# Block 2's query-key products added over chunks on GpSimd, values ahead of the second softmax, and three blocks' outputs added to x by accumulating DMA

## The chip, the cores and the metric

The kernel runs on one core of a Trainium2 chip. The core has five engines with instruction streams of their own: TensorE (PE: matrix products, with weight loads listed as PEld), VectorE (DVE), ScalarE (ACT), GpSimd (POOL) and SyncE (SP, which here only issues DMAs). SBUF is the on-chip memory of 128 partitions; PSUM holds 8 banks of 128 x 512 float32 in which PE leaves its results. The metric is the device time of one execution in microseconds; a smaller one is better. The median of the runs of the kernel before is 271.93 us.

## The reference

The batch is 1, S = 2048 positions, D = 640 channels, H = 32 heads of Dh = 20, W = 8 offsets, F = 1536 hidden channels, all bf16. Two branches work on the same normalised x, and both are added to x:

```python
def _A_ref(x, wqkv, wo):
    q, k, v = heads(x @ wqkv)          # each [B, H, S, Dh]
    off = jnp.arange(8) * 2
    idx = pos[:, None] - off[None, :]
    ...
    logits = jnp.einsum("bhsd,bhswd->bhsw", q, kg) * scale
    logits = jnp.where(mask[None, None, :, :], logits, -1e9)
    attn = _softmax(logits, axis=-1)
    o = jnp.einsum("bhsw,bhswd->bhsd", attn, vg)
    return o.transpose(0, 2, 1, 3).reshape(B, S, D) @ wo

def _B_ref(x, w_gate, w_up, w_down):
    g = jnp.einsum("bsd,df->bsf", x, w_gate)
    u = jnp.einsum("bsd,df->bsf", x, w_up)
    return jnp.einsum("bsf,fd->bsd", g * u, w_down)

xn = _layernorm(x, axis=-1)
return x + _A_ref(xn, A_wqkv, A_wo) + _B_ref(xn, B_w_gate, B_w_up, B_w_down)
```

So each position attends to eight earlier positions of its own head, two apart, and a gated product without a nonlinearity runs beside it.

## The kernel before

The 2048 positions are cut into NJ = 4 blocks j of 512, each block into 4 tiles of 128 positions (16 tiles t in all). The 640 channels are NCH = 5 chunks c of 128, and the hidden channels are NF = 12 tiles m of 128. Data lies transposed, channels on partitions, positions along the free axis.

**How the order is made.** The code does not emit instructions in the order in which it is written. Each stage is a Python generator that yields conditions (`have`, `num`: a mark or a count has been reached) and Tasks (engine, priority, banks needed). A planner keeps a model time for each engine and picks the next Task per engine by priority; what it picks is the fixed order of that engine's instructions. On the chip semaphores enforce only the data dependencies. Each engine works strictly in that order: an instruction that waits holds up all that stand behind it. `occ` and `acc` are the planner's assumed durations, and `prio` its priorities.

**The stages**, with the names that the instructions bear:

1. Front: LayerNorm of the 16 tiles, transposed by DMA into XNT.
2. Projections (L671, L703): q into `p0_...`, k into `p1_...`, v into `pv...`; values go to a scratch tensor in DRAM (`vst`) and come back shifted as VX (`vx_loads`, 4 DMAs for each of the 20 units u = (block, chunk)).
3. Query-key products. `QUAD`, at L415, says which blocks take the wide way. The narrow way (L835, products at L846, `prod`) multiplies a chunk of q by four shifted views of k on DVE, 128 x 2048 in bf16: two such instructions (r = 1, 0) for each chunk. The wide way (L876) is used for chunks 0 to 3 of a block: DVE multiplies q, read from a PSUM bank, by two shifted views into float32, 128 x 1024 (L893, `prow`), and the four chunks are added into one: by POOL adds (L919 `qsum`, L937 `qend`) and by accumulating DMAs from SBUF to SBUF issued by POOL (L915; `BY_DMA` names the two of four per pair of chunks). For a block on the wide way that is 16 half-products, 8 POOL adds and 4 DMAs. Chunk 4 always goes the narrow way. In before, block 3 alone is wide.
4. Logits (L944): matmuls at L959 sum over the 20 channels of each head with the small selector G, 32 output rows at a time, four column groups side by side. A narrow block needs 2 x 5 x 4 = 40 of them, a wide one 16.
5. Softmax over the eight offsets, L986, in two halves: x = 0 for blocks 0 and 1, x = 1 for blocks 2 and 3, on DVE with the exponential on ACT (L1007) and the last multiply `attn` at L1016; then 16 small DMAs move the weights into ATX0 or ATX1.
6. Weighted values (L1077, L1093): for each unit two multiplies on DVE (L1131, `pv`) into float32 PV, each followed by one add on POOL (L1136, `pva`) into an SV slot; then a selector matmul on PE over all units of a batch (L1174, matmuls at L1184, named I0 to I19), evicted into OT by ACT (L1193). `BATCH`, L1049, lists the last unit of each batch. First and last chunks of a block are multiplied in halves, because ACT must replace the weights in PSUM between blocks (L1091).
7. Gate and up (`gu`, L1206): 5 matmuls for each of 12 tiles m, twice, per block (L1235); ACT evicts the gate (L676), DVE multiplies by the up bank (L1244, `h`), or ACT evicts both and POOL multiplies (L1261, `hp`). Results lie in HT for blocks 0 and 1, in HX for block 2 and in XNT for block 3 (`ht`).
8. Down and output projection (`dn`, L1290, L1302): for each tile t and each half row, 12 matmuls over the hidden tiles and 5 over OT into one bank (L1317); DVE adds x from XR (L1330, `fin`) into FOUT, and SP stores the row. XR is loaded by `xr_loads` (L1278), three slots in turn.

Where PE would have nothing to do in attention, the planner fills it with stage 7. The selector matmuls of stages 4 and 6 run in a mode with four column groups; all others use the whole array.

Of the kernel before, what the change touches and what calls it, by code (L numbers as in the profile page):

```python
# [6 lines left out]
ALU = mybir.AluOpType  # L7
# [13 lines left out]
NJ = 4  # L21
# [327 lines left out]
def build_kernel(nc, A_x, A_wqkv, A_wo, B_x, B_w_gate, B_w_up, B_w_down, out):  # L349
# [39 lines left out]
    NS = 5  # L389
    SV = [sb(f"SV{i}", [128, 4, JB], at=a_pr + i * 4096) for i in range(3)]  # L390
    SV += [sb("SV3", [128, 4, JB], at=a_qk + 33024), sb("SV4", [128, 4, JB], at=a_qk + 33024 + 4096)]
    SV += [sb(f"SV{5 + i}", [128, 4, JB], at=a_ra + i * 4096) for i in range(3)]
    sv_free = [3, 4, 0, 1, 2]
    a_sc = place[0]
    place[0] += 8192
# [16 lines left out]
    NPR = len(PRD)  # L412
    PRD += [sb("PRD12", [128, 4, JB], at=a_sc), sb("PRD13", [128, 4, JB], at=a_sc + 4096)]
    PRD32 = [K.sbuf(f"PRF{i}", [128, 2, JB], FP32, K.base[p.name]) for i, p in enumerate(PRD)]
    QUAD = {3: (1, 0)}  # L415
    BY_DMA = (((0, 0), (0, 2)), ((1, 0), (1, 2)))
    NXR = 3
    a_xr = place[0]
    XR = sb("XR", [128, NXR, D])
    FOUT = sb("FOUT", [128, 2, D])  # L420
    NXN = 5
    XNS = sb("XNS", [128, NXN, D], at=a_xr)
    NUX = 3
# [14 lines left out]
    def ht(j, m):  # L438
        if j == 3:
            return XNT[:, m % NCH, m // NCH * JB:(m // NCH + 1) * JB]  # L440
        return HX[HXM[m]][:] if j == 2 else HT[:, j, m, :]

    HXM = (0, 1, 2, 3, 8, 9, 10, 11, 4, 5, 6, 7)
    WPOS = (2, 0, 1)
# [57 lines left out]
    def loads():  # L502
        def t(f, *a):
            return Task("sp", lambda: f(*a), prio=0)

        for t_ in range(3, NXS):
            yield t(x_load, t_)
        yield t(wqkv_load, 2)
        for t_ in range(NXS, NT):
            yield have("apply", t_ - NXS)  # L510
            yield t(x_load, t_)

        def w(T, src):
            dma(T[:], src.rearrange("(c p) n -> p c n", p=128), w=[T[:]], name="ld_w")

        def pads():
            z = ZERO[:, 0:PAD].unsqueeze(1).to_broadcast([128, NCH, PAD])
            dma(vscr[:, 0:PAD].rearrange("(c p) s -> p c s", p=128), z, r=[ZERO[:, 0:PAD]], w=[("vscr", "pad")], name="vpad")

        yield have("xnt", NT - 1)  # L520
        yield t(w, WG, B_w_gate)
        yield t(pads)
        yield t(w, WU, B_w_up)

    def late_loads():
        yield num(NJ, "lg")
# [519 lines left out]
        yield Task("sp", move, r=[L[:]], prio=4)  # L1046

    NU = NJ * NCH
    BATCH = (4, 9, 14, 19)  # L1049

    def vx_loads():
        yield have("products")
# [121 lines left out]
    def sums(us):  # L1174
        hold = []
        for u in us:
            yield have("add", u)

        def go(*bs):
            hold.extend(bs)  # L1180
            for u, b in zip(us, bs):
                for dq in range(4):
                    o, p = PS[32 * dq:32 * dq + 32, b, :], SV[sv_of[u]][:, dq, :]
                    op("pe", (lambda o, p, dq: lambda e: e.matmul(o, SEL[:], p, start=True, stop=True,  # L1184
                                                                 tile_position=(0, 32 * dq)))(o, p, dq),
                       r=[SEL[:], p], w=[o], name=f"I{u}_{dq}", occ=0.054, lat=0.4, mode=1)
                sv_free.append(sv_of[u])

        def ev():
            for u, b in zip(us, hold):  # L1190
                j, c = divmod(u, NCH)
                o = OT[:, j, c, :]
                X = op("act", (lambda o, b: lambda e: e.activation(o, PS[:, b, :], ACT.Copy))(o, b), r=[PS[:, b, :]], w=[o],  # L1193
                       name=f"oev{u}", occ=0.58)
                K.free_bank(b, X)
                bump("ot", j)

        yield Task("pe", go, r=[SV[sv_of[u]][:] for u in us], prio=9.7, banks=len(us), slack=0.7)
        yield Task("act", ev, r=[PS[:, b, :] for b in hold], prio=3)
# [6 lines left out]
    def gu(j):  # L1206
        if j == 0:
            for m in range(NCH):
                for jj in range(NJ):
                    yield num(4, "qk", 1, jj, m)  # L1210
            for jj in range(NJ):
                yield num(NCH, "v", jj)
        elif j == 1:
            for m in range(NCH):
                for jj in range(NJ):
                    yield num(4, "qk", 0, jj, m)
        elif j == 2:
            yield have("atx", 0)
        if j:
            yield have("gu", j - 1)  # L1220
        for m in range(NF):
            h = ht(j, m)
            if j == 1 and m == 6:
                yield num(NJ - 1, "lg")
            if j == 2 and m == 4:
                yield num(NJ, "lg")
            if j == 2 and m == 8:
                yield have("atx", 1)
            hold = []

            def go(which, b):
                T = (WG, WU)[which]
                for c in range(NCH):
                    l, x = T[:, c, m * 128:(m + 1) * 128], XNT[:, c, j * JB:(j + 1) * JB]
                    op("pe", (lambda l, x, c: lambda e: e.matmul(PS[:, b, :], l, x, start=(c == 0), stop=(c == NCH - 1)))(l, x, c),  # L1235
                       r=[l, x], w=[PS[:, b, :]], name=f"gu{which}_{m}_{j}_{c}", occ=0.2158, lat=0.3)
                hold.append(b)

            def after(h=h, hold=hold, j=j, m=m):
                def ev():  # L1240
                    K.free_bank(hold[0], evac([(h, PS[:, hold[0], :], JB)], f"gev{m}_{j}"))

                def mul():
                    X = op("dve", lambda e: e.tensor_tensor(h, h, PS[:, hold[1], :], ALU.mult), r=[h, PS[:, hold[1], :]],  # L1244
                           w=[h], name=f"h{m}_{j}", occ=0.65)
                    K.free_bank(hold[1], X)
                    bump("h", j)

                yield Task("act", ev, r=[PS[:, hold[0], :]], w=[h], prio=7)
                yield lambda: len(hold) > 1  # L1250
                if on_pool(j, m):
                    k = ucount[0] % NUX
                    k0 = ucount[0]
                    ucount[0] += 1
                    us = UX[:, k, :]

                    def uev():
                        K.free_bank(hold[1], evac([(us, PS[:, hold[1], :], JB)], f"uev{m}_{j}"))

                    def pmul():  # L1260
                        op("pool", lambda e: e.tensor_tensor(h, h, us, ALU.mult), r=[h, us], w=[h], name=f"hp{m}_{j}",  # L1261
                           occ=1.15, lock=True)
                        bump("hp")
                        bump("h", j)

                    yield Task("act", uev, r=[PS[:, hold[1], :]], w=[us], prio=7)
                    yield num(k0, "hp")
                    yield room(1.15)
                    yield Task("pool", pmul, r=[h, us], w=[h], prio=HP_PRIO, lock=True)
                    return  # L1270
                yield Task("dve", mul, r=[h, PS[:, hold[1], :]], prio=H_PRIO)

            yield Task("pe", lambda b: go(0, b), prio=50, banks=1, keep=GU_KEEP, r=[WG[:]])
            K.spawn(after())
            yield Task("pe", lambda b: go(1, b), prio=49, banks=1, keep=GU_KEEP - 1, r=[WU[:]])
        mark("gu", j)

    def xr_loads():  # L1278
        yield num(NJ, "lg")
        yield have("vx", NVX)  # L1280
        for t in range(NT):
            if t >= NXR:
                yield have("out", t - NXR)
            yield Task("sp", lambda: dma(XR[:, t % NXR, :], xhbm[t * TS:(t + 1) * TS, :], w=[XR[:, t % NXR, :]], name=f"xr{t}"),
                       prio=15, w=[XR[:, t % NXR, :]])
            mark("xr", t)

    stores = []
# [1 line left out]
    def dn(j):  # L1290
# [3 lines left out]
        for st in range(4):  # L1294
            t = 4 * j + st
            pieces = ((0, 320), (320, 480), (480, 640)) if t == NT - 1 else ((0, 320), (320, 640))
            yield have("xr", t)
            yield lambda: count.get(("ot", j), 0) >= NCH or ("gu", NJ - 1) in done
            for nb, (c0, c1) in enumerate(pieces):
                yield from dn_piece(j, t, nb, slice(st * TS, (st + 1) * TS), c0, c1)  # L1300
# [1 line left out]
    def dn_piece(j, t, nb, rows, c0, c1):  # L1302
# [1 line left out]
        wid = c1 - c0  # L1304
        hold = []
        n = NF + NCH
        o, xr = FOUT[:, t % 2, cols], XR[:, t % NXR, cols]

        def part(lo, hi):
            b = hold[0]  # L1310
# [17 lines left out]
        def fin():  # L1328
# [2 lines left out]
                   name=f"fin{t}_{nb}", occ=0.15 + wid / 960)  # L1331
            K.free_bank(b, X)

        def store():
            if t == NT - 1:
                f, d = o, ohbm[t * TS:(t + 1) * TS, cols]
            else:
                f, d = FOUT[:, t % 2, :], ohbm[t * TS:(t + 1) * TS, :]
            stores.append(dma(d, f, r=[f], name=f"odma{t}_{nb}", eng="act" if nb == 1 and t == NT - 1 else "sp"))

        def tail():
            yield num(NCH, "ot", j)
            yield Task("pe", rest, r=[OT[:, j, :, rows]], prio=40)
            yield Task("dve", fin, r=[PS[:, hold[0], :], xr], w=[o], prio=FIN_PRIO)
            if nb == 1 or t == NT - 1:
                yield Task("act" if nb == 1 and t == NT - 1 else "sp", store, r=[o], prio=9)
# [13 lines left out]
    FIRST = 9  # L1360
    GU_KEEP = 3
    HP_MAX = 2
    ORDER = ((0, "n"), (1, "n"), (2, "n"), (3, "n"), (3, "w"))
    LAST = ORDER[-1][0]
    HP_PRIO = 30
    DN_KEEP = 3
# [79 lines left out]
```

## Time and profile before

| what | value |
|---|---|
| runs of before | 271.67, 271.93, 272.11 us, median 271.93 |
| the profiled execution, its own time | 271.67 us |
| its span | 270.1 us |
| mean granted TensorE clock | 1.0 |
| matmuls L1235 (gate, up), x469 | 116.9 us busy |
| matmuls L1317 (down, output), x357 | 55.0 us busy |
| POOL adds of values L1136 x40 | 93.9 us, mean 2.367 |
| POOL multiplies L1261 | 16 before the last value add, 1.12 to 1.17 us each |
| DVE multiplies of values L1131 x54 | 91.6 us, 2.279 whole and 1.215 half |
| DVE half-products L893 x16 | 18.9 us, mean 1.217 |
| DVE bf16 products L846 x32 | 36.7 us, one taking 1.219 in the mean |
| DVE output adds L1330 x33 | 15.6 us |
| last value add on POOL ends | 239.12 us |
| PE's last matmul ends | 267.36 us |

The span is what the profile covers; 1.57 us of the execution's own time lie around it. Start times are in us from the span's start. In a row of a group the columns are: line, engine, operation, output and inputs with their shapes, count; then the busy time and the mean ns of one; then the idle time just ahead of the group's instructions and what ended most of it. A matmul's end is modelled, and matmuls are pipelined, so the pace (the distance from one start to the next) is the number to use for PE: 1.079 us for a group of five, 2.31 for a piece of 17 with 320 columns.

### The profile page before, as it was taken

The numbers are of one execution on the slowest core, as the hardware profiler recorded it, in microseconds if no ns is written. First come the engines' busy times: TensorE is split into PE (matmuls) and PEld (weight loads), VectorE is DVE, ScalarE is ACT, GpSimd is POOL, SyncE is SP. The second block draws the span as 40 slices with busy tenths as digits, with TensorE's granted clock in tenths as the row PEclk, the third lists the DMA queues.
The fourth block names the chain that finished last, engine by engine and source line by source line (L and its number), as shares of the span: only waits on it lengthen the run. The fifth ranks groups of instructions, "written<-read, shape, count | busy, mean of one in ns | idle before, by whom it ended". The sixth has DMA issues, their size and how long they took to land.

```text
span 270.1 us, 4455 instructions
## 1 busy us (share of the span) xinstructions
PE 261.8 (97%) x1771; PEld 152.5 (56%) x1788; DVE 214.4 (79%) x254; ACT 109.3 (40%) x194; POOL 142.0 (53%) x95
## 2 busy tenths in 40 slices
PE   7999999999998999999899999999999999999996
PEld 5986964544443444444344577446764577544775
DVE  4687899999986989599996979979998999711221
ACT  3459986558524222435534500453006500365000
POOL 3000000000062289993379998799986999775000
PEclk9999999999999999999999999999999999999999
DMA  7964679602429992895222836633567311300101
GB/s 228 368 186 88 125 133 402 209 0 96 124 50 209 224 226 72 247 280 120 57 47 49 201 107 170 182 98 81 146 173 192 80 49 55 93 0 2 49 27 49
DMA packets 40933, 35.75 MB, mean 132 GB/s; under 512 B 16080, under 2 KB 39120, under 8 KB 40912
## 3 DMA queue, kind: packets, MB, share of 16 engines
q1 hardware_dynamic: 40096, 33.31, 45.6%
q0 software_dynamic: 576, 2.10, 3.9%
q8 instruction: 14, 0.23, 0.4%
q10 hardware_dynamic: 240, 0.05, 0.1%
q14 instruction: 7, 0.06, 0.1%
HBM read 25.07 MB, written 5.26 MB: 112 GB/s over the span
## 4 chain that ended last, share of the span: by engine, by line
PE 72%; DVE 9%; ACT 6%; POOL 5%; SPq 3%; issue 2%; DMA 2%; DVEq 0%
PE PS L1235 30%; PE PS L1317 27%; PE PS L671 9%; DVE PRD L846 4%; POOL SV L1136 3%; SPq L467 3%; ACT XNS L582 3%; PE PS L703 2%; PE PS L1184 1%; PE PS L959 1%; DMA XST<-in_A_x_dram 1%; DVE SM L989 1%; DVE LOG L1016 1%; POOL HT L1261 1%; DVE PV L1131 1%
## 5 line engine op out<-in xcount | busy, mean ns | idle before, releaser
L1136 POOL TENSOR_TENSOR SV<-PV 128x1024 bf16<-128x1024 f32 x40 | 93.9, 2367 | 13.8 <-DVE PV L1131 12.1
L1131 DVE TENSOR_TENSOR PV<-VX,PS 128x1024 f32<-128x1024 bf16 (+1 forms) x54 | 91.6, 1727 | 5.8 <-POOL SV L1136 3.9
L671 PE MATMUL PS<-XNT,WQKV 128*128 128x512 bf16 (+2 forms) x384 | 59.8, 315 | 1.7 <-ACT HT L676 1.1
L1235 PE MATMUL PS<-XNT,WG 128*128 128x512 bf16 x237 | 59.0, 379 | 0.5 <-DVE HT L1244 0.2
L1235 PE MATMUL PS<-XNT,WU 128*128 128x512 bf16 x232 | 57.9, 379 | 0.9 <-ACT HT L676 0.5
L671 PEld LDWEIGHTS PS<-XNT,WQKV 128*128 128x128 bf16 x390 | 37.7, 113 | 23.4 <-ACT HT L676 1.6
L1235 PEld LDWEIGHTS PS<-XNT,WU 128*128 128x128 bf16 x240 | 23.2, 98 | 29.3 <-ACT HT L676 1.0
L1235 PEld LDWEIGHTS PS<-XNT,WG 128*128 128x128 bf16 x240 | 23.3, 98 | 28.6 <-DVE HT L1244 0.7
L846 DVE TENSOR_TENSOR PRD<-QT,KT 128x2048 bf16<-128x2048 bf16 x32 | 36.7, 1219 | 0.0
L1330 DVE TENSOR_TENSOR FOUT<-PS,XR 128x320 bf16<-128x320 f32 (+1 forms) x33 | 15.6, 477 | 17.8 <-PE PS L1317 17.7
L1317 PE MATMUL PS<-WD,HT 128*128 128x320 bf16 x192 | 28.4, 299 | 0.0
L1317 PE MATMUL PS<-WO,OT 128*128 128x320 bf16 (+1 forms) x165 | 26.6, 295 | 0.0
L919 POOL TENSOR_TENSOR PRF<-PRF,PRF 128x1024 f32<-128x1024 f32 x4 | 9.4, 2356 | 29.3 <-DVE PRF L893 29.3
L978 POOL MEMSET LOG<- 32x6 bf16 (+6 forms) x7 | 0.4, 95 | 44.1 <-ACT LOG L970 44.1
L1317 PEld LDWEIGHTS PS<-WD,HT 128*128 128x128 bf16 x192 | 18.6, 98 | 7.8 <-DVE HX L1244 0.4
L676 ACT ACTIVATE HT<-PS 128x512 bf16<-128x512 f32 x24 | 13.8, 594 | 22.5 <-PE PS L1235 22.5
L676 ACT ACTIVATE UX<-PS 128x512 bf16<-128x512 f32 x21 | 12.6, 600 | 25.4 <-PE PS L1235 23.5
L893 DVE TENSOR_TENSOR PRF<-PS,KT 128x1024 f32<-128x1024 f32 x16 | 18.9, 1217 | 0.8 <-DMA PRF<-PRF 0.8
L1317 PEld LDWEIGHTS PS<-WO,OT 128*128 128x128 bf16 x165 | 15.9, 98 | 5.9
L676 ACT ACTIVATE HX<-PS 128x512 bf16<-128x512 f32 x12 | 7.2, 597 | 26.7 <-PE PS L1235 26.6
L676 ACT ACTIVATE XNT<-PS 128x512 bf16<-128x512 f32 x12 | 7.2, 597 | 24.9 <-PE PS L1235 24.9
L1244 DVE TENSOR_TENSOR HT<-HT,PS 128x512 bf16<-128x512 bf16 x20 | 13.4, 681 | 4.6 <-ACT HT L676 3.3
(63 smaller groups left out, 248.6 us busy)
## 6 DMA issues: line engine op xcount, KB each, us to landing
VX<-v_scratch SPq DMA_DIRECT2D x80, 130.0 KB, 2.9
XST<-in_A_x_dram SPq DMA_DIRECT2D x16, 160.0 KB, 5.7
v_scratch<-VST SPq DMA_DIRECT2D x4, 640.0 KB, 5.4
XR<-in_A_x_dram SPq DMA_DIRECT2D x16, 160.0 KB, 2.8
out_dram<-FOUT SPq DMA_DIRECT2D x15, 160.0 KB, 2.0
PRF<-PRF POOLq DMA_DIRECT2D x4, 512.0 KB, 8.7
WG<-in_B_w_gate_dram SPq DMA_DIRECT2D x1, 1920.0 KB, 7.7
WU<-in_B_w_up_dram SPq DMA_DIRECT2D x1, 1920.0 KB, 11.5
```

The lines of the kernel that those rows point to most:

```text
L467: return op(eng, lambda e: e.dma_start(o, i), r=r, w=w, dma=True, name=name, nbytes=n, group=group, land=land)
L671: op("pe", (lambda o, l, x, c, first: lambda e: e.matmul(o, l, x, start=first, stop=(c == NCH - 1)))(o, l, x, c, first), r=[l, x], w=[o], ...
L676: X = op("act", (lambda o, i: lambda e: e.activation(o, i, ACT.Copy))(o, i), r=[i], w=[o], name=name, occ=0.12 + n * 0.9e-3)
L846: op("dve", lambda e: e.tensor_tensor(s[:], qb, kv, ALU.mult), r=[q, rk], w=[s[:]], name=f"prod{j}_{r}_{c}", occ=1.15, lock=True)
L893: X = op("dve", lambda e: e.tensor_tensor(o[:], qb, kv, ALU.mult), r=[q, rk, ("qev", j, c)], w=[o[:]], name=f"prow{j}_{r}_{c}_{q0}", occ=1.17)
L919: yield Task("pool", lambda: op("pool", lambda e: e.tensor_tensor(x, x, y, ALU.add), r=[x, y] + tokens(), w=[x], name=name, occ=2.36, lock ...
L1131: op("dve", lambda e: e.tensor_tensor(p, vw, a, ALU.mult), r=[vv] + rk, w=[p], name=f"pv{u}_{x}_{r0}", occ=0.09 + 1.1 * nr)
L1136: X = op("pool", lambda e: e.tensor_tensor(o, p[:, :, 0, :], p[:, :, 1, :], ALU.add), r=[p[:]] + tokens(), w=[o], name=f"pva{u}_{x}", occ= ...
L1235: op("pe", (lambda l, x, c: lambda e: e.matmul(PS[:, b, :], l, x, start=(c == 0), stop=(c == NCH - 1)))(l, x, c), r=[l, x], w=[PS[:, b, :] ...
L1244: X = op("dve", lambda e: e.tensor_tensor(h, h, PS[:, hold[1], :], ALU.mult), r=[h, PS[:, hold[1], :]], w=[h], name=f"h{m}_{j}", occ=0.65)
L1317: op("pe", (lambda l, x, i: lambda e: e.matmul(dst, l, x, start=(i == 0), stop=(i == n - 1)))(l, x, i), r=[l, x], w=[PS[:, b, :]], name=f" ...
L1330: X = op("dve", lambda e: e.tensor_tensor(o, PS[:, b, 0:wid], xr, ALU.add), r=[PS[:, b, :], xr], w=[o], name=f"fin{t}_{nb}", occ=0.15 + wi ...
```

## The change

Four things change together.

- **Block 2 takes the wide way too.** `QUAD` gets block 2, and `ORDER` plans block 2's wide part ahead of block 3's. Block 2 loses 8 of its 10 narrow products and 24 of its 40 logit matmuls, and gets 16 half-products, 8 POOL adds and 4 accumulating DMAs. One narrow pair per block stays (chunk 4).
- **Outputs of blocks 0 to 2.** x is no longer added on DVE. Early on, one DMA on SP copies rows 0 to 1535 of x into the output (`copy_x`, planned after the second block's logits; in SP's order it stands between the stores of values of block 0 and block 1, ahead of the loads of ATX). For blocks 0 to 2 ACT evicts each half row from PSUM into FB0, and when a block's eight pieces are there, one DMA issued by POOL adds the block of 512 rows to the output (`add_out`, `accum_op=add`). Block 3 keeps the way of before (FB1, XR). XR is loaded for block 3's four tiles only, once block 0's down pieces are planned, and SP stores rows of block 3 alone.
- **Batches.** The units' sums go in seven batches instead of four (`BATCH`). Block 3's batches wait until the down pieces of block 2 are planned.
- **Places in SBUF.** Block 2's last four hidden tiles use block 3's OT instead of slots that wait for softmax 2's move, so the wait `have("atx", 1)` of `gu(2)` is gone; SV has six slots instead of eight; the buffers of the outputs move.

In the fixed orders that come out, PE has seven batches of small matmuls for the units: I0, I1 inside block 2's hidden tiles, I2 to I4 after the gate of tile 3 of block 3, then I5 and I6 between down tiles 1 and 2, I7 to I9, I10 and I11, I12 to I14 and I15 to I19 among the further down tiles. Block 2's logits stand after the up product of tile 10 of block 0, block 3's after the gate of tile 11 of block 1. On POOL, all sums of block 2 stand ahead of block 3's, and these ahead of the first value add; eight `hp` stand ahead of the last value add where there were 16, and the three output DMAs stand between the two adds of units 9, 14 and 19.

```diff
-    SV += [sb(f"SV{5 + i}", [128, 4, JB], at=a_ra + i * 4096) for i in range(3)]
+    SV += [sb("SV5", [128, 4, JB], at=a_ra + 6 * D * 2)]
...
-    QUAD = {3: (1, 0)}
+    QUAD = {2: (1, 0), 3: (1, 0)}
     BY_DMA = (((0, 0), (0, 2)), ((1, 0), (1, 2)))
-    NXR = 3
     a_xr = place[0]
-    XR = sb("XR", [128, NXR, D])
-    FOUT = sb("FOUT", [128, 2, D])
+    FB0 = sb("FB0", [128, 5, D])
+    FB1 = sb("FB1", [128, 2, D], at=a_ra)
+    XR = sb("XR", [128, 4, D], at=a_ra + 2 * D * 2)
...
-        return HX[HXM[m]][:] if j == 2 else HT[:, j, m, :]
+        if j == 2:
+            return OT[:, 3, m - 8, :] if m >= 8 else HX[HXM[m]][:]
+        return HT[:, j, m, :]
...
+        def copy_x():
+            a, b = ohbm[0:3 * JB, :], xhbm[0:3 * JB, :]
+            o, i = a.rearrange("(p r) n -> p (r n)", p=128), b.rearrange("(p r) n -> p (r n)", p=128)
+            op("sp", lambda e: e.dma_start(o, i), w=[("outx",)], dma=True, name="outx", nbytes=2e6)
+
+        yield num(2, "lg")
+        yield t(copy_x)
...
-    BATCH = (4, 9, 14, 19)
+    BATCH = (1, 4, 6, 9, 11, 14, 19)
...
+        if us[-1] >= 3 * NCH:
+            yield num(8, "dn", 2)
...
-            if j == 2 and m == 8:
-                yield have("atx", 1)
...
-        yield num(NJ, "lg")
-        yield have("vx", NVX)
-        for t in range(NT):
-            if t >= NXR:
-                yield have("out", t - NXR)
+        yield num(8, "dn", 0)
+        for st in range(4):
+            t = 12 + st
...
-            yield have("xr", t)
+            if j == 3:
+                yield have("xr", t)
...
-        o, xr = FOUT[:, t % 2, cols], XR[:, t % NXR, cols]
+        F, ft = (FB1, t % 2) if j == 3 else (FB0, t % 4)
+        o, xr = F[:, ft, cols], XR[:, t % 4, cols]
...
+        def fin_act():
+            K.free_bank(hold[0], evac([(o, PS[:, hold[0], 0:wid], wid)], f"fin{t}_{nb}"))
+            bump("fin", j)
+            if count["fin", j] == 8:
+                K.one(Task("pool", add_out, r=[F[:, 0:4, :]], prio=5))
+
+        def add_out():
+            d = ohbm[j * JB:(j + 1) * JB, :].rearrange("(t p) n -> p t n", p=128)
+            f = F[:, 0:4, :]
+            stores.append(op("pool", lambda e: e.dma_start(d, f, accum_op=ALU.add), r=[f, ("outx",)], w=[("out", j)], dma=True,
+                             name=f"oadd{j}", occ=0.88, acc=4))
...
+            if j < 3:
+                yield Task("act", fin_act, r=[PS[:, hold[0], :]], w=[o], prio=6)
+                return
...
-    ORDER = ((0, "n"), (1, "n"), (2, "n"), (3, "n"), (3, "w"))
+    ORDER = ((0, "n"), (1, "n"), (2, "n"), (3, "n"), (2, "w"), (3, "w"))
```

More of the change, by code (lines that the diff above doesn't have):

```diff
@@ L1278, in xr_loads @@
     def xr_loads():
-        yield num(NJ, "lg")
-        yield have("vx", NVX)
-        for t in range(NT):
-            if t >= NXR:
-                yield have("out", t - NXR)
-            yield Task("sp", lambda: dma(XR[:, t % NXR, :], xhbm[t * TS:(t + 1) * TS, :], w=[XR[:, t % NXR, :]], name=f"xr{t}"),
-                       prio=15, w=[XR[:, t % NXR, :]])
+        yield num(8, "dn", 0)
+        for st in range(4):
+            t = 12 + st
+            yield Task("sp", lambda: dma(XR[:, st, :], xhbm[t * TS:(t + 1) * TS, :], w=[XR[:, st, :]], name=f"xr{t}"),
+                       prio=15, w=[XR[:, st, :]])
             mark("xr", t)
@@ L1337, in store @@
             else:
-                f, d = FOUT[:, t % 2, :], ohbm[t * TS:(t + 1) * TS, :]
+                f, d = F[:, ft, :], ohbm[t * TS:(t + 1) * TS, :]
             stores.append(dma(d, f, r=[f], name=f"odma{t}_{nb}", eng="act" if nb == 1 and t == NT - 1 else "sp"))
```

## The prediction, made before the change ran

> **What bounds the kernel now.** I read the busy totals first, then the chain that ended last, then windows of that chain's stages (length, then busy us of PE, PE's weight loads, DVE, ACT and POOL, the granted clock, the DMA share, GB/s).
>
> ```profile
> PE 261.8 (97%) x1771; PEld 152.5 (56%) x1788; DVE 214.4 (79%) x254; ACT 109.3 (40%) x194; POOL 142.0 (53%) x95
> PE 72%; DVE 9%; ACT 6%; POOL 5%; SPq 3%; issue 2%; DMA 2%; DVEq 0%
> 35.00:84.00 49.00, 47.33 (x306) 22.98 (x310) 45.55 (x44) 29.78 (x51) 5.05 (x9) 1.00 0.49 153
> 130.00:151.00 21.00, 19.69 (x102) 8.23 (x103) 18.56 (x18) 11.62 (x22) 16.78 (x10) 1.00 0.30 71
> 151.00:249.00 98.00, 97.63 (x644) 58.53 (x647) 77.61 (x69) 28.89 (x53) 87.10 (x46) 1.00 0.41 107
> ```
>
> PE is the bound, at full granted clock. So a change pays only by taking matmuls or gaps out of PE, and costs only where it makes PE wait. After 151 PE has no gap to lose, but POOL is busy 87.1 of 98 us there: it is the next bound. Before 84 POOL is nearly empty (5.05 of 49). PE's few gaps stand in the chain of waits (start, duration, what) and in the timelines:
>
> ```profile
> 45.12 2.27 PE PS L959 x40
> 79.92 1.93 DMA ATX<-LOG
> 81.88 1.12 ACT PS L1091 x2
> 82.99 0.53 ACT HT L676
> 83.56 2.35 PE PS L671 x10
> 111.82 0.98 PE PS L959 x16
> ...
> 136.48 1.15 DVE LOG L1016
> 137.69 4.67 POOL SV L1136 x2
> ```
> ```profile
> 117.92 3.61 DVE L989 TENSOR_TENSOR M<-M 128x512 bf16<-128x512 bf16 x2
> 126.11 3.00 DVE L989 TENSOR_TENSOR SM<-LOG 128x1024 f32<-128x1024 bf16 x1
> 150.38 0.39 PE L1184 MATMUL PS<-SV,SEL 128*32 128x512 bf16 x2 [0.61 <-POOL SV L1136]
> ```
>
> PE stood 1.56 us before 83.56 (softmax 1's weights go by DMA, then two ACT copies, then the eviction that PE needs), 0.98, 0.65 and 0.47 at 131 to 136.5 (its banks wait for DVE, which is in softmax 2), and 1.10 inside the batch of five units' sums near 150 (unit 4's last add on POOL ends 150.32). The matmuls after each gap run a little denser: a block-by-block sum from 83.56 to the end (94 groups of five at 1.079, 33 down pieces at 2.31 less two halves, 96 small ones) leaves 2.1 us of real loss in 183.8.
>
> **The change, part by part.**
>
> *Logits.* A block multiplied in bf16 costs 40 small matmuls (2.27), a block added over chunks 16 (0.98). Block 2 goes from 40 to 16: PE saves 1.3. The batch also moves behind 83.56, so that PE fills the time before it with two groups more.
>
> *Block 2 on DVE and POOL.* Eight products of 128x2048 bf16 (pace 1.137 in a run, mean 1.219) become sixteen half-products of the same price: +9.1 us of DVE, between 69 and 110, where DVE is the fullest engine after PE (45.55 of 49 before 84). What is late by it are the hidden multiplies (0.6 each), and behind them PE's banks; their cover is that the half-products now wait for POOL's buffers, and DVE goes to the multiplies in between. Without that cover one bank would be late by one half-product, 1.1. POOL gets eight more adds and four more accumulating DMAs:
>
> ```profile
> L919 POOL TENSOR_TENSOR PRF<-PRF,PRF 128x1024 f32<-128x1024 f32 x4 | 9.4, 2356 | 29.3 <-DVE PRF L893 29.3
> L915 POOL DMA_DIRECT2D PRF<-PRF x4 | 3.6, 892 | 9.9 <-DVE PRF L893 7.9 <-DMA PRF<-PRF 2.0
> L1131 DVE TENSOR_TENSOR PV<-VX,PS 128x2048 f32<-128x2048 bf16 x26 | 59.1, 2279 | 1.7 <-POOL SV L1136 1.7
> ```
>
> 8 x 2.32 (pace) + 4 x 0.89 = 22.1 of POOL, from 68.95 (the first softmax's end). With the landings (8.3 to 9.4, median 8.7), as block 3 shows them (76.95 to 109.86, which is 32.9, some 2 of it a landing awaited, and DVE's blocks of multiplies in it), block 2 ends near 99.4, 2.4 sooner than that analogy (101.8), because three half-products are made inside the first softmax, ahead of its last operation, and POOL can start at once. PE comes to its logits at 83.56 + 16 groups x 1.079 = 100.8. Covered by 1.4, and late by 1.1 if the analogy holds in full. Block 3's adds then start at 99.4 and are paced by its half-products on DVE (the last near 115): end near 128.7; PE is there after 27 groups and a logit batch more, at 130.9. Covered by 2.2. I take no new gap at the logits, but POOL reaches its first value add 19 us later: unit 0's ends near 131.0, against 112.2.
>
> *Values and softmax 2.* Unit 1's second product ends 5.1 after that add (117.3 now, 136.3 then, with a pending multiply between). From it to the end of the second softmax DVE takes 20.3 now; one product more, 2.2, lies between: 136.3 + 22.5 = 158.8 against 137.62. If the two blocked operations above (3.61 for two, 3.00 for one, against 1.2 in the first softmax) run free because POOL waits meanwhile, 3 us come back: 156 to 160; I take 159, nearest to the row.
>
> From there to unit 4's last add now takes 12.6, with three GpSimd multiplies of 1.12; with two, 11.5: 170.5. PE wants it at 167.8: 83.56 + 75 groups x 1.079 + two logit batches (1.96) + the batch of units 0 and 1 (0.73) + the entry and first two units of the next (0.6). A gap of 2.7, in which the old ones at 131 and 150 are gone. Behind it on PE stand 17 groups (18.3), 33 down pieces (73.8) and 60 small matmuls in five batches (4.7): 96.9. So PE ends at 170.9 + 96.9 = 267.8 against 267.36: +0.5. Without that gap it would be 265.2.
>
> *Seven batches for four.* Entering and leaving the small-matmul mode costs 0.42 gaps on either side, part of which the denser next group gives back: 0.3 net, so +0.9, counted above. The Trainium skill, page "TensorEngine Tiling (Array Packing)", Key Properties, says that changing the tiling mode drains TensorE. This speaks against the change and agrees with the 0.42 seen; by the rule without the give-back three batches would cost 2.5 rather than 0.9.
>
> *POOL from unit 5 to 19.* 30 adds x 2.32 = 69.6, four multiplies (4.5), three issues of the new output DMA. Rows for such an issue: 0.84 to 1.00 for 128 rows of 4 KB. The new one has 512 rows of 1,280 B: if the price goes by call 0.9, if by row 3.5. I take 1.0, near the row, and keep 0.84 to 3.5. Sum 77.1; plus the gaps in which POOL now waits for DVE at block borders (0.23 three times, 1.41, 0.46, 0.23: 2.8), of which I take half, since fins leave DVE: 1.4. Unit 19's add: 170.5 + 78.5 = 249.0. PE wants it at 170.9 + 78.2 = 249.1. In balance, with 0.7 to 1.5 of slack at the earlier batches without the border gaps. I put +0.5 for what of them shows. The output DMA is followed on POOL by the second add of units 9, 14 and 19; it waits for eight ACT copies and the copy of x, both early, so nothing stands long behind it.
>
> *Outputs.* 24 of DVE's 31 half-row adds of 0.487 (11.7 us) become ACT evictions (0.39 for 128x256, about 0.45 here: 11). ACT is busy 28.9 of 98, so hidden; if it were late, PE's next bank would be. SP loses 23 issues. The copy of x rows 0 to 1535 (1.97 MB) goes out on SP after the second logits, ahead of the value stores and the ATX moves; its landing lies under 80 us of other work. Its issue and bandwidth could push the ATX0 wait at 83.56 by 0 to 1; nearest row: 1.9 MB of weights land in 11.5. That delay would be swallowed by the gap at unit 4: 0. The first eviction of block 1 waits for block 0's output DMA to have read its buffer; there are 13 us of cover by the 8.7 landing. Last fins and stores are as now (2.74 after PE's end).
>
> The Trainium skill, page "SBUF — State Buffer", section "Who interferes with whom", says that a VectorE operation with two SBUF inputs and a GpSimd one that reads SBUF exclude each other. The rows 3.61 and 3.00 fit that. Here DVE gets 16 more of the PSUM-fed kind, which the rule lets pass; without the rule their 1.217 beside POOL's 2.36 says the same.
>
> **Sum.** Against the profiled execution (271.67, span 270.1): +0.5 +0.5, and 0.3 for issue and border together = +1.3, so 273.0. The median shown is 271.93.
>
> **Rivals.**
> 1. *Softmax 2 comes early enough.* If attention's last operation ends at or before 156.2 (no blocking by POOL, block 3's adds denser), unit 4's gap goes and POOL gains as much. 271.67 - 2.1 = 269.6, with half the border cost 270.1. For: 6.6 us in the two blocked rows. Against: POOL still adds values through the same softmax.
> 2. *The output DMA's issue is the new bound.* Its place is POOL between units 9, 14 and 19. At 3.5 each it costs 7.5 more than reckoned, against a slack of 0.1 at unit 19; it decides from 1.2 per issue on. At 2.0: +3.0, so 276; at 3.5: 280. For: four times as many rows. Against: no such row in the trace.
> 3. *Block 2's adds or the copy of x make the logits late.* Slack 1.4: if the landings go from 8.7 to 11 with 2 MB more traffic, block 2's sums, block 3's and softmax 2 shift by 2 to 4, and the gap at unit 4 with them: 275.
> 4. *Balance.* Gains and gaps meet within 0.5: 271.7.
>
> **How the numbers follow.** Forecast 0.42, rival 1 0.25, rival 2 0.10, rival 3 0.11, balance 0.12. The likeliest has its own range of 272.2 to 274.2. With rival 1's times and rivals 2 and 3 to 276 the range is 270.0 to 276.0; beyond it, below 270.0 about 0.1 and above 276.0 about 0.1. A measurement of this kernel tells 0.2% (0.54 us) from no change. Faster: rival 1 and a little of balance, 0.27. Same: balance and the forecast's lower edge, 0.15. Slower: the rest, 0.58.
>
> **What would show it.** Right: PE idle at 131 to 136 gone, a gap of 2 to 3 before unit 4's sums released by POOL, attention's end near 159, POOL's last value add near 249, the block logits with 16 matmuls without a wait, and an issue of the output DMA near 1.0. Wrong: no gap at unit 4 (rival 1), POOL busy over 2 us in an output issue (rival 2), PE waiting at logits 2 or 3 for POOL (rival 3), or a new gap at 83.56 beyond 2.6.

## The result, and the profile after

| kernel | median, us | runs | lowest to highest |
|---|---|---|---|
| before | 272.02 | 4 | 271.67 to 272.43 |
| changed | 282.06 | 4 | 280.63 to 282.35 |

The ratio is 1.0358, with a 95% interval of 1.0319 to 1.0397: the change costs some 10 us. The forecast was 273.0 with a range of 270.0 to 276.0, so it missed. The profiled execution of the changed kernel took 280.63, with a span of 278.8; its span is 8.7 longer than that of before.

The page of the changed kernel, its busy line, the slices of the granted clock and the line of the chain by engine:

```profile
PE 262.9 (94%) x1747; PEld 151.8 (54%) x1764; DVE 221.1 (79%) x249; ACT 111.8 (40%) x203; POOL 155.6 (56%) x99
PEclk9999999999997799999999999999999999999999
PE 65%; DVE 14%; SPq 6%; ACT 5%; POOL 4%; DMA 3%; issue 2%; DVEq 0%
```

PE's busy time is 1.1 us up, though it has 24 matmuls less to do: two slices ran at a lower clock. In the chain, PE's share fell from 72% to 65%, and SP's queue went from 3% to 6%. The chain around those slices (start, duration, what):

```profile
69.10 0.73 SPq L469
...
85.23 3.78 DMA ATX<-LOG
89.03 1.12 ACT PS L1101 x2
90.15 0.52 ACT HT L686
...
90.72 10.26 PE PS L1245 x40
...
109.61 0.98 PE PS L969 x16
```

This is the chain that stood before the 1.56 us gap at 83.56, link by link, but 7.2 us later: the 16 moves into ATX0, two copies on ACT, one eviction, and PE. The gap in before's timeline (1.56 is read between PE's weight loads; between its matmuls it is 1.07):

```profile
83.56 1.88 PEld L671 LDWEIGHTS PS<-XNT,WQKV 128*128 128x128 bf16 x10 [1.56 <-ACT HT L676]
```

Two timelines of the changed kernel show where the 7.2 us arise, first ACT, then SP and POOL:

```profile
77.09 0.60 ACT L686 ACTIVATE HT<-PS 128x512 bf16<-128x512 f32 x1 [3.72 <-PE PS L1245]
89.03 1.12 ACT L1101 ACTIVATE PS<-ATX 128x512 f32<-128x512 bf16 x2 [11.34 <-DMA ATX<-LOG]
90.09 1.06 ACT L686 ACTIVATE HT<-PS 128x512 bf16<-128x512 f32 x2
```
```profile
69.10 17.51 SPq L469 DMA_DIRECT2D ATX<-LOG  x16
73.77 1.03 POOL L925 DMA_DIRECT2D PRF<-PRF  x1
75.04 0.85 POOL L925 DMA_DIRECT2D PRF<-PRF  x1 [0.24 <-DVE PRF L903]
78.13 0.84 POOL L925 DMA_DIRECT2D PRF<-PRF  x1 [2.24 <-DVE PRF L903]
81.49 0.85 POOL L925 DMA_DIRECT2D PRF<-PRF  x1 [2.52 <-DVE PRF L903]
```

ACT stood 11.34 us at a copy whose result DVE first uses at 128.7 (the first value product). Behind the copies in ACT's order stood the eviction of gate tile 2, for which PE waited 8.27 us (between matmuls). SP spent 17.51 us on the 16 moves; before it was 11.21:

```profile
69.31 11.21 SPq L467 DMA_DIRECT2D ATX<-LOG  x16
```

The four DMAs that block 2 adds on POOL fall into just this stretch. In before, the DMAs of block 3 were issued from 85.7 on, when the moves had landed (at 81.9):

```profile
85.69 1.00 POOL L915 DMA_DIRECT2D PRF<-PRF  x1 [4.07 <-DVE PRF L893]
```

The windows of the stage (length, then busy us of PE, weight loads, DVE, ACT, POOL, then granted clock, DMA share, GB/s), of after:

```profile
84.00:130.00 46.00, 39.02 (x184) 17.68 (x188) 34.37 (x37) 12.16 (x21) 28.27 (x15) 0.93 0.61 124
```

In before, PE was busy for 45.74 us there, at a clock of 1.00. The two terms that make the loss are the later start (90.72 against 83.56: 7.2) and the slow matmuls right behind it (40 in 10.26 us, where 40 x 0.216 = 8.64: 1.6). 7.2 + 1.6 = 8.8, against 8.7 in the span; all else that the change does adds up to nothing.

In three of the four runs of the changed kernel the mean granted clock was 0.982 and not the 0.988 of the profiled one, and these took 1.2 to 1.7 us more, which the last section comes back to.

### The profile page after: what moved, and what is told of

Same layout as the page of the kernel before. It is cut to its first block, busy times and chain, and to the rows that moved or that the text cites. A ratio compares the mean times of both kernels' runs of the same rounds, so it can differ in the third digit from the quotient of the medians.

```text
span 278.8 us, 4404 instructions
## 1 busy us (share of the span) xinstructions
PE 262.9 (94%) x1747; PEld 151.8 (54%) x1764; DVE 221.1 (79%) x249; ACT 111.8 (40%) x203; POOL 155.6 (56%) x99
## 4 chain that ended last, share of the span: by engine, by line
PE 65%; DVE 14%; SPq 6%; ACT 5%; POOL 4%; DMA 3%; issue 2%; DVEq 0%
PE PS L1327 27%; PE PS L1245 26%; PE PS L681 8%; SPq L469 6%; DVE PRD L856 4%; POOL SV L1146 3%; ACT XNS L592 3%; DVE SM L999 2%; DVE PV L1141 2%; PE PS L713 2%; PE PS L1196 2%; DMA XST<-in_A_x_dram 1%; DMA ATX<-LOG 1%; PE PS L969 1%; DVE PRF L903 1%
## 5 line engine op out<-in xcount | busy, mean ns | idle before, releaser
L1146 POOL TENSOR_TENSOR SV<-PV 128x1024 bf16<-128x1024 f32 x40 | 96.5, 2674 | 12.5 <-DVE LOG L1026 7.8
L1245 PE MATMUL PS<-XNT,WU 128*128 128x512 bf16 x236 | 59.2, 381 | 0.4 <-issue 0.3
L903 DVE TENSOR_TENSOR PRF<-PS,KT 128x1024 f32<-128x1024 f32 x32 | 37.9, 1217 | 0.3 <-PE PS L681 0.3
L929 POOL TENSOR_TENSOR PRF<-PRF,PRF 128x1024 f32<-128x1024 f32 x8 | 18.8, 2358 | 32.0 <-DVE LOG L1026 20.7
L1254 DVE TENSOR_TENSOR HT<-HT,PS 128x512 bf16<-128x512 bf16 x24 | 16.4, 685 | 17.9 <-ACT HT L686 9.5
L856 DVE TENSOR_TENSOR PRD<-QT,KT 128x2048 bf16<-128x2048 bf16 x24 | 27.3, 1222 | 0.0
L686 ACT ACTIVATE FB<-PS 128x320 bf16<-128x320 f32 x24 | 10.5, 438 | 40.1 <-PE PS L1327 40.1
L947 POOL TENSOR_TENSOR PRD<-PRF,PRF 128x1024 bf16<-128x1024 f32 x8 | 18.7, 2357 | 1.6 <-DVE PRF L903 1.6
L1340 DVE TENSOR_TENSOR FB<-PS,XR 128x320 bf16<-128x320 f32 (+1 forms) x9 | 4.1, 455 | 15.4 <-PE PS L1327 15.4
L557 DVE BATCH_NORM_STATS2 STATS<-XST 128x6 f32<-128x320 bf16 x32 | 14.1, 471 | 2.4 <-DMA XST<-in_A_x_dram 2.3
```

The source lines that it names most:

```text
L686: X = op("act", (lambda o, i: lambda e: e.activation(o, i, ACT.Copy))(o, i), r=[i], w=[o], name=name, occ=0.12 + n * 0.9e-3)
L856: op("dve", lambda e: e.tensor_tensor(s[:], qb, kv, ALU.mult), r=[q, rk], w=[s[:]], name=f"prod{j}_{r}_{c}", occ=1.15, lock=True)
L903: X = op("dve", lambda e: e.tensor_tensor(o[:], qb, kv, ALU.mult), r=[q, rk, ("qev", j, c)], w=[o[:]], name=f"prow{j}_{r}_{c}_{q0}", occ=1.17)
L929: yield Task("pool", lambda: op("pool", lambda e: e.tensor_tensor(x, x, y, ALU.add), r=[x, y] + tokens(), w=[x], name=name, occ=2.36, lock ...
L947: yield Task("pool", lambda: op("pool", lambda e: e.tensor_tensor(o, a, y, ALU.add), r=[a, y] + tokens(), w=[o], name=f"qend{j}_{r}_{q0}", ...
L1146: X = op("pool", lambda e: e.tensor_tensor(o, p[:, :, 0, :], p[:, :, 1, :], ALU.add), r=[p[:]] + tokens(), w=[o], name=f"pva{u}_{x}", occ= ...
```

## The experiments

Each was compared with the kernel before on the same chip (medians of before between 272.16 and 272.35). "Copies" are the two ACT instructions at L1101, named atp0_0 and atp0_1, which bring softmax 1's weights into PSUM.

| run | edit against | median, us | ratio to before, 95% |
|---|---|---|---|
| e1_copies_later | changed | 270.66 | 0.9956 (0.9936 to 0.9976) |
| e2_sums_on_pool | changed | 272.35 | 1.0000 (0.9976 to 1.0023) |
| e3_x_copied_later | changed | 281.97 | 1.0351 (1.0309 to 1.0394) |
| e4_before_copies_later | before | 270.34 | 0.9928 (0.9911 to 0.9945) |
| e5_filler | changed | 279.85 | 1.0278 (1.0241 to 1.0314) |
| e6_block3_wide_alone | changed | 272.78 | 1.0023 (1.0013 to 1.0032) |
| e7_no_pool_multiplies | e1 | 268.28 | 0.9854 (0.9838 to 0.9871) |
| e8_units_later | e1 | 271.27 | 0.9984 (0.9965 to 1.0002) |
| e9_before_no_pool_multiplies | before | 268.25 | 0.9854 (0.9835 to 0.9873) |
| e10_block3_wide_no_pool_multiplies | changed | 269.25 | 0.9892 (0.9875 to 0.9909) |
| e11_five_batches | e7 | 267.77 | 0.9836 (0.9819 to 0.9854) |

**e1: does PE stand because of ACT's order?** After planning, the two copies are moved within ACT's list; no other order changes.

```diff
     K.run()
+    at = [X for X in K.ops if X.name in ("atp0_0", "atp0_1")]
+    K.ops = [X for X in K.ops if X not in at]
+    i = [X.name for X in K.ops].index("gev11_0")
+    K.ops[i:i] = at
     K.emit(stores)
```

> The changed kernel with the two ACT copies of softmax 1's weights moved, in ACT's order alone, from ahead of the eviction of gate tile 2 to behind block 2's logits; all else in the same order. Theory (the 8.3 us stand of PE at 82.4 comes from ACT's order: the copies wait for the late ATX0 moves and hold up the evictions behind them): no stand there, no low clock after it, PE at block 2's logits near 99, end near 271 (269.5 to 274, since POOL's sums of block 2 may be late by some us). Rival (PE stands there for work that is late itself, the half-products or the banks): PE stands at the same place or within 10 us behind it for nearly as long, 278 to 282.

It took 270.66, 11.4 less than the changed kernel. The ATX0 moves were nearly as slow as in the changed kernel (16.58 us, the last of them issued at 84.06), but nothing that PE needs waited for them. ACT's timeline of this run at the place of the 11.34 us:

```profile
76.92 0.60 ACT L686 ACTIVATE HT<-PS 128x512 bf16<-128x512 f32 x1 [3.72 <-PE PS L1245]
79.08 0.60 ACT L686 ACTIVATE HT<-PS 128x512 bf16<-128x512 f32 x1 [1.56 <-PE PS L1245]
...
101.11 1.12 ACT L1101 ACTIVATE PS<-ATX 128x512 f32<-128x512 bf16 x2
```

ACT now waits for PE and no longer the other way, and the copies at 101.11 wait for nothing. So the late moves cost time only through the place of the copies.

**e2 and e3: what made the moves late?** In e2 block 2's four accumulating DMAs become POOL adds in the same places:

```diff
+            if j == 2:
+                X = K.ops[-1]
+                X.dma, X.needs_tick, X.event = False, True, None
+                X.fn = lambda e: e.tensor_tensor(x, x, y, ALU.add)
```

> The changed kernel with the four accumulating DMAs of block 2 replaced by four POOL adds in the same places of the same orders; block 3's stay. Theory (these DMAs run beside the ATX0 moves and slow them: 16 moves take 17.5 us to issue and land at 89.0 instead of 81.9): the moves issue at 0.60 to 0.65 each and land near 82, PE stands 1 to 2 us, then loses 2 to 5 at block 2's logits since POOL has 5.9 us more: 274 to 278. Rival (the copy of x, or the stores of values, slow the moves): they land at 88 to 89 again and the time is 282 or more.

In e3 the copy of x goes out later, behind the first loads of VX:

```diff
-        yield num(2, "lg")
+        yield num(NJ, "lg")
         yield t(copy_x)
```

> The changed kernel with the copy of x into the output moved on SP from ahead of the second store of values to behind the first loads of VX; all other orders the same. Theory (accumulating DMAs slow the moves): ATX0 lands at 88 to 89 as now, 281 to 283. Rival (the 2 MB copy ahead of the moves slows them): ATX0 lands near 82 and the time is 272 to 274.

SP's timeline of e2, then that of e3:

```profile
69.09 11.10 SPq L469 DMA_DIRECT2D ATX<-LOG  x16
```
```profile
68.80 17.60 SPq L469 DMA_DIRECT2D ATX<-LOG  x16
```

Without block 2's DMAs the moves take 11.10 us, as in before; without the copy of x ahead of them they take 17.60, as in the changed kernel. Block 2's accumulating DMAs are the cause, and the copy of x has no part in it. Nor have the stores of values, which e2 leaves where they were. In e2 PE went on at 83.19, and the time was 272.35. The expected 2 to 5 us of waiting at block 2's logits did not come: POOL's last sum of block 2 ended at 99.18 and PE was there at 100.56, because without landings to await the adds ran almost on end (2.0 us of idle time from 69.1 to 99.2). So at block 2's logits the four transfers gained nothing.

**e4: the same wait in before.** The same edit, with the copies put ahead of gate tile 6.

```diff
+    i = [X.name for X in K.ops].index("gev6_0")
```

> The kernel before with the two ACT copies of softmax 1's weights moved in ACT's order from ahead of the eviction of gate tile 0 to ahead of that of gate tile 6. Theory (the 1.56 us stand of PE at 83.56 is the same wait in small): that stand goes, 270.3 to 270.8. Rival (the time is given back at the next wait for POOL near 111 or 131): 271.7 to 272.2.

270.34: the 1.56 us stand, small in before, was the same wait, and its removal is kept to the end.

**e5: what is the 1.6 us behind the stand?** 36 matmuls whose results are not used fill the stand.

```diff
+        X.fn = lambda e: e.matmul(PS[:, at_bank[0], :], WG[:, 0, 0:128], XNT[:, 0, 0:JB], start=True, stop=True)
```

> The changed kernel with 36 matmuls more on PE (128x512, 7.8 us at the pace of 0.216) behind the up product of tile 2 of block 0, into a bank that nobody uses then; so PE works through most of its stand, and its results are not used. Theory (the slow matmuls behind the stand, 10.26 us for 40 instead of 8.6, come of PE having stood idle): PE stands less than 2 us, 40 matmuls behind it take 8.6 to 8.9, granted clock 1.0 there, and the time falls by 1.5 to 3 below the changed kernel's: 279 to 280.5, though nothing waits less. Rival (the clock falls for another reason, such as the transfers of that stretch): the matmuls stay slow, 282 or more.

The chain of e5 behind the stand, PE's first 4 matmuls and the 40 after these:

```profile
90.70 1.04 PE PS L1247 x4
...
91.79 8.80 PE PS L1247 x40
```

PE goes on at 90.70, within 0.02 us of the changed kernel, but at full speed (granted clock 1.00 from 84 to 98, against 0.76). The end comes 2.2 us earlier (279.85 against 282.06; 1.6 between the profiled runs, 279.00 against 280.63) although PE does 7.8 us more work. So the slow matmuls come of PE having been idle.

**e6 and e10: what is block 2's wide way worth?** Block 3 alone is wide, the rest of the change stays, the copies stand later; in e10 all hidden multiplies are on DVE too. The orders are planned anew.

```diff
-    QUAD = {2: (1, 0), 3: (1, 0)}
+    QUAD = {3: (1, 0)}
-    ORDER = ((0, "n"), (1, "n"), (2, "n"), (3, "n"), (2, "w"), (3, "w"))
+    ORDER = ((0, "n"), (1, "n"), (2, "n"), (3, "n"), (3, "w"))
```

> The changed kernel with block 3 alone on the wide way (as before the change) and the two copies of softmax 1's weights behind gate tile 5 in ACT's order; the outputs by accumulating DMA and the seven batches stay. The orders are planned anew. Theory (block 2's wide way gains 1.3 on PE and gives it back by POOL, whose value adds start 19 us later and then leave PE 0.2 to 0.8 of slack at each batch): no stand at unit 4 from POOL's late start, first value add near 110, 269.5 to 271. Rival (the wide way of block 2 is a net gain): over 271.5.

272.78: this expectation failed, and the rival holds. Against e1 (270.66) block 2's wide way gains 2.1, though e6's orders were planned anew and e1's were not. PE's timeline of e6 shows the stands:

```profile
122.40 1.25 PE L1245 MATMUL PS<-XNT,WU 128*128 128x512 bf16 x5 [0.38 <-DVE HT L1254]
124.23 1.25 PE L1245 MATMUL PS<-XNT,WG 128*128 128x512 bf16 x5 [0.58 <-ACT HT L686]
131.51 1.25 PE L1245 MATMUL PS<-XNT,WG 128*128 128x512 bf16 x5 [0.63 <-ACT HT L686]
150.78 0.39 PE L1196 MATMUL PS<-SV,SEL 128*32 128x512 bf16 x2 [1.08 <-POOL SV L1146]
```

Softmax 2 runs beside POOL's value adds, as in before, and the stands of before come back; that the one causes the other is not shown. Two of them are the ACT pattern again. In e6's ACT timeline, evictions stand behind an instruction that waits for softmax 2 on DVE:

```profile
121.78 1.91 ACT L1017 ACTIVATE LOG<-LOG 128x2048 bf16<-128x2048 bf16 x1 [3.98 <-DVE LOG L1012]
123.60 1.07 ACT L686 ACTIVATE HT<-PS 128x512 bf16<-128x512 f32 x2
...
130.10 0.42 ACT L1021 ACTIVATE SM<-SM 128x256 f32<-128x256 f32 x1 [3.98 <-DVE SM L999]
130.55 0.42 ACT L1022 ACTIVATE RS<-SM 128x256 bf16<-128x256 f32 x1
130.88 1.55 ACT L686 ACTIVATE HT<-PS 128x512 bf16<-128x512 f32 x3
```

Before has the same at 130.32, where ACT waited 3.63 us for the softmax's sum.

**e7, e8: what bounds the mended kernel?** e7 takes the multiplies from POOL (the copies stay late). e8 keeps them and moves the sums of units 2 to 4 on PE, behind 2.7 us of other work. The first two lines are e7's edit, the others e8's.

```diff
-    HP_MAX = 2
+    HP_MAX = 0
...
+    us = [X for X in lists["pe"] if X.name.split("_")[0] in ("I2", "I3", "I4")]
+    lists["pe"] = [X for X in lists["pe"] if X not in us]
+    i = [X.name for X in lists["pe"]].index("dn0_0_11") + 1
+    lists["pe"][i:i] = us
```

> The changed kernel with the copies behind block 2's logits, and all hidden multiplies on DVE (ten of 1.12 us leave POOL, ten of 0.6 come to DVE); planned anew. Theory (with the copies out of the way POOL is the bound from softmax 2 on: a stand of 2.1 at unit 4 and nothing to spare later): the stand shrinks to under 0.5 and the time falls by 1.5 to 2.5 below 270.7: 268.2 to 269.2. Rival (DVE becomes the bound, or the stand follows softmax 2 whatever POOL does): 270.2 or more.

> The kernel of the first experiment (copies behind block 2's logits) with the sums of units 2, 3 and 4 moved on PE alone behind the next up product and the first twelve matmuls of the first down piece (2.7 us of work), so that the 2.1 us stand at unit 4 is filled. Theory (from there on PE runs into POOL's value adds again: slack of 0.4, 0.8, 0.8, 0.7 and 0.3 at the five later batches): most of the 2.1 comes back as waits at those batches, 270.1 to 270.7. Rival (those adds would not be late): 268.4 to 269.2.

e7 came out as expected, at 268.28, but not for the reason given. Its unit 4's last add still ended at 168.98 (169.04 in e1), with POOL now idle for 3.43 us before unit 4's adds. PE's stand shrank from 2.12 to 0.61 us (between weight loads; between matmuls it was 1.82 in e1), because the new order has two groups more ahead of the sums. Its window shows the engine that is full:

```profile
130.00:170.00 40.00, 39.57 (x205) 17.34 (x199) 39.90 (x38) 17.14 (x30) 20.86 (x9) 1.00 0.55 136
```

DVE is busy 39.90 of 40 us, POOL 20.86. In e1, where the multiplies are still on POOL, the chain from the end of softmax 2 (157.44) to unit 4 is POOL's:

```profile
157.52 4.67 POOL SV L1146 x2
162.19 1.11 POOL HX L1271
163.31 1.11 POOL OT L1271
164.42 4.63 POOL SV L1146 x2
169.05 0.04 issue
169.10 0.39 PE PS L1196 x2
```

So up to the end of softmax 2 it is DVE that bounds, and from there to unit 4 POOL. Moving the multiplies ends softmax 2 earlier, at 152.85, but then DVE is the bound up to unit 4, which comes no sooner. In e8 the stand did not go, it moved:

```profile
169.64 1.80 PE L1327 MATMUL PS<-WD,HT 128*128 128x320 bf16 x12 [2.32 <-DVE XNT L1254]
```

PE now waits 2.32 us for a hidden multiply of DVE (168.90), and that stands in DVE's order behind value multiplies that had waited 1.03 us for an add on POOL. 271.27 is neither of the two expected times, and at the later batches PE waited for POOL no more (it sums unit 6 at 180.66, POOL had it at 179.29). So half of the theory fell: POOL leaves PE slack behind unit 4. From softmax 2 to unit 4 POOL bounds e1 and e8, with DVE close behind, and DVE bounds e7.

**e9: both edits on before,** the copies ahead of gate tile 6 and `HP_MAX` at 0.

```diff
-    HP_MAX = 2
+    HP_MAX = 0
...
+    i = [X.name for X in K.ops].index("gev6_0")
```

> The kernel before with the two copies ahead of gate tile 6 in ACT's order, and all hidden multiplies on DVE instead of 17 or more on POOL; planned anew. Theory (in the kernel before it is DVE, in softmax 2 and with the output adds still on it, that holds PE's banks; more multiplies there cost): 271 to 274, slower than with the multiplies on POOL (270.3). Rival (POOL's load is what holds both kernels): under 270, as with the changed kernel.

268.25, so the theory fell here too: taking the multiplies off POOL helps before by 2.1 (270.34 to 268.25), as it helps the changed kernel by 2.4 (270.66 to 268.28). From 58.7 on no gap between PE's weight loads is longer than the 0.42 to 0.43 that stand at each entry into and exit from the small-matmul mode. Why multiplies on POOL cost before so much isn't settled: the order was planned anew, and no run separates the new order from the engine.

With before and the changed kernel now equal (268.25 and 268.28), e10 asks what the halves of the change are worth in this state. It is e6 with `HP_MAX` at 0.

> The changed kernel with block 3 alone wide, the copies behind gate tile 5 and no hidden multiplies on POOL; planned anew. With the kernel before under the same two edits at 268.25 and the changed one at 268.28 this tells apart what the two halves of the change are worth once nothing stands in ACT's order. Theory (PE is then without stands, and only its own work counts): three batches more than the kernel before, at 0.3 each: 269.0 to 269.4; block 2's wide way then gains its 1.3 less what unit 4 costs (0.6). Rival (the outputs by accumulating DMA gain or cost something themselves): under 268.5 or over 270.

269.25, as expected: with no stands left, outputs by DMA and seven batches cost 1.0 against e9, about the 0.9 expected for three batches, and block 2's wide way gains 1.0 against e10 (268.28 in e7). No run has the outputs without the batches, so that the output DMAs themselves cost nothing is inferred.

**e11: fewer batches.**

```diff
-    BATCH = (1, 4, 6, 9, 11, 14, 19)
+    BATCH = (1, 4, 9, 14, 19)
```

> The changed kernel with the copies behind block 2's logits, no hidden multiplies on POOL and five batches of units (last units 1, 4, 9, 14, 19) instead of seven; planned anew. Theory (each batch costs PE 0.3 and the seven were not needed): 267.5 to 267.9. Rival (fewer batches make the sums wait, since only six slots are there): 268.3 or more.

267.77: two batches fewer gain 0.5, and this is the fastest version here. The gain is small: its slowest run (267.96) lies below the fastest of e9 (268.03) and e7 (268.09), but the 95% intervals of the three ratios overlap.

## Why the prediction was wrong, point by point

**The step that failed.** Block 2's accumulating DMAs were priced on POOL alone, as 4 x 0.89 of issue and a landing. What else is in flight when they run was not asked. The prediction looked at the ATX0 moves only for the copy of x, "0 to 1", from a row of weights that land in 11.5. The copy had landed by 58.4, ten us ahead of the moves, and e3 shows its share to be nothing. With the DMAs the last of the 16 moves was issued at 85.23 instead of 79.92, and it landed 3.8 us after that instead of 1.9: together the 7.2. Before's own trace held the warning: the chain of waits that the prediction quotes runs through these moves, and its own term put the new DMAs from 69 on, the time at which the moves start.

**"That delay would be swallowed by the gap at unit 4: 0."** This was wrong by itself. The changed kernel has both the 8.27 stand and a stand of 2.12 at unit 4, the same 2.12 as e1 and e2. DVE and POOL live on what PE produces: while PE stood they ran dry too (both were busy 0.00 us from 82.5 to 90.7), and softmax 2 ended 10 us later (167.53 against 157.44 in e1). A wait is swallowed only by the slack of work that doesn't depend on it.

**The clock.** A stand of several us was counted at its length. It cost 1.6 more in the profiled run, and more again in the three runs with a mean clock of 0.982.

**Rivals.** Rival 3 named the traffic, but placed it in the sums' own landings, which fell from 8.7 to 5.2. The list of signs held "a new gap at 83.56 beyond 2.6", and that is what came. One reading of before missed the order of ACT too: the prediction put the 0.98 gap near 131 down to DVE alone, but PE waited there for an eviction on ACT that stood behind the wait at 130.32.

**What held.** e1 lacks the stand altogether and in e2 it is 1.23 us (1.56 in before, both between weight loads), so they show the other steps without the new delay:

| step | predicted | e1 | e2 |
|---|---|---|---|
| PE at block 2's logits, us | 100.8 | 99.5 | 100.6 |
| PE at block 3's logits | 130.9 | 129.7 | 130.8 |
| softmax 2 ends | 158.8 | 157.4 | 158.5 |
| unit 4's last add ends | 170.5 | 169.0 | 170.1 |
| stand at unit 4 | 2.7 | 2.1 | 2.1 |
| unit 19's last add ends | 249.0 | 246.7 | 249.2 |
| time | 273.0 | 270.7 | 272.4 |

Up to unit 4, e1 is 1.2 to 1.5 ahead of the prediction and 1.1 ahead of e2, because the old stand went with the new one. In the changed kernel the output DMAs kept POOL for 0.82 to 0.84 each (the first from 202.13 to the next add at 202.97), so rival 2 falls: 512 rows cost what 128 did. The outputs on ACT were hidden, as said (0.4 us of waiting for them in all); e10 and e11 fit the 0.3 for each batch, 1.0 for three and 0.5 for two. That POOL is the next bound held in e1 from softmax 2 to unit 4, 11.5 us as added up; what the prediction did not see is how close DVE is, which is full (39.90 of 40 us) as soon as POOL's multiplies move to it.

## What to carry to other kernels

Price a new DMA also by what it runs beside: look up which transfers are in flight in the stretch where it lands, and whether an engine in order waits for one of them. An early instruction that waits for a DMA, put ahead of evictions in an engine's fixed order, makes every delay of that DMA a stand of PE; standing it behind work that is ready cost nothing here and gained 11.4 and 2.0 us. Two kernels that seem to differ by a part can be equal once a shared wait is out of the way, so mend the wait first and then compare the parts.

## What the runs showed of the hardware that was not expected

**Accumulating DMAs slow other queues' issue.** In e2, without block 2's transfers, 14 of SP's 16 moves of 32 KB took 0.60 or 0.61 us to issue, the others 0.72 and 1.31. With four transfers of 512 KB issued by POOL between 73.8 and 82.3, the last eight took 0.91 to 1.58. (The longest, 1.83, is the sixth, which began before the first of the transfers and is also the long one in e2.) The Trainium skill's page "DMA: Bandwidth & Descriptors", section "Issuing engines are not separate DMA queues", says that DMAs of all issuing engines run on the same 16 engines and interleave. The comparison of e2 with the changed kernel fits that; here it was 6.4 us on the issue of 16 moves (17.51 against 11.10). Whether plain transfers of the same size would do the same, no run tells.

**The clock drops by stretches of time, and not always.** Behind the 8.27 stand seven matmuls came 0.40 to 0.43 us apart, then at 0.216; the granted clock was 0.50 from 86.9 to 93.6, so it had fallen while PE still stood. In e3's profile it was 0.50 from 86.5 to 96.5, and that run took 281.91 us; its mean clock, 0.982, is that of the changed kernel's three longer runs. The Trainium skill, "TensorE: Matmul & The Clock Gate", section "What's actually happening", puts a half-speed clock behind an idle window of about 3.4 us, and says that the window runs freely. The 0.43 fits the half speed. The stand of 2.12 at unit 4 is shorter than that window, and yet it can cost more than its length: in e1 four of ten runs had a mean clock of 0.994 and took 271.9 to 272.1, and six had 1.0 and took 270.4 to 270.8. The profile of e2 caught it behind the stand; the granted clock was 0.50 from 170.2 to 173.5, and 0.89 in this window:

```profile
165.00:180.00 15.00, 13.12 (x78) 7.03 (x78) 13.95 (x10) 4.85 (x10) 15.00 (x8) 0.89 0.45 111
```

The kernels without such a stand (e7, e9, e10, e11) kept a clock of 0.999 or 1.0 in every run whose clock is on record. So the stand of 2.12 costs its length, or some 1.6 us more, by the run.
